# RWKV-6 attention with a tanh-shrink MLP on one core: in the boot, two state sums move from VectorE to ScalarE and GpSimd, and two weight loads are issued later

## The chip, the core and the metric

The kernel runs on one core of a Trainium2 chip. The core has five engines that run beside each other and wait for each other through semaphores: TensorE (PE, matrix products; the loading of its weights is listed apart as PEld), VectorE (DVE), ScalarE (ACT), GpSimd (POOL) and SyncE (SP, which here only issues DMAs). The metric is the device time of one execution in microseconds. Before the change it is 544.36 us, the median of 3 runs (544.14 to 544.81).

## The reference

Two stages follow each other. The first is an RWKV-6 attention over 4 batches, 8 heads, 768 tokens and a head width of 48; the second an MLP on the 3072 x 384 matrix that it makes.

```python
for t in range(S):
    cur = np.einsum('bhd,bhe->bhde', u[None] * kt, vt)
    y[:, :, t] = np.einsum('bhd,bhde->bhe', rt, state + cur)
    state = wt[:, :, :, None] * state + np.einsum('bhd,bhe->bhde', kt, vt)
...
x = y.transpose(0, 2, 1, 3).reshape(B * S, H * D)     # 3072 x 384
h = x @ w_in                                          # 384 x 2048
g = h - np.tanh(h)
return g @ w_out                                      # 2048 x 384
```

## The kernel before

**Tiling.** The 3072 tokens are cut into 8 blocks of 384 (four batches, two halves `q` of each). In a block the attention works in 6 chunks of 64 tokens. The 8 heads are held as 4 pairs, and the pairs as two halves, `h1` (pairs 2 and 3) and `h2` (pairs 0 and 1). Inside a chunk the result comes from scores (`from_scores`, L698: values by a masked matrix A), across chunks from states (`from_states`, L679). The results are copied out of PSUM by `result_out` (L741) into `xT0` to `xT2`, the transposed input of the MLP. Each xT takes 96 of its 128 rows from one pair; the other 32 rows, the "holes", come from the fourth pair, which is first copied to a tile `late` and then spread by six small DMAs (`fill_holes`, L789: half of them issued by SyncE, half by GpSimd, two for each xT).

**The MLP.** It runs in 16 rounds `f` for each block: TensorE multiplies xT by a 128-column slice of `w_in` (`first`, L883), ScalarE copies the product out of PSUM (L888), ScalarE and VectorE work out h - tanh h, and TensorE multiplies by a slice of `w_out`. Round 0 takes xT2 first, then xT1, then xT0. While TensorE does this for one block, the other engines prepare the attention of the next.

**The weights** arrive as 64-bit words, in 16 raw loads of 768 KB (`load_weights`, L251, five buffers). Each one is turned into float32 by three ScalarE pieces (L264: one writes `w_sb`, two write `up`) and one VectorE piece (L268). The order of loads is fixed by `UNITS`: the first raw load holds `w_in` for rounds 0 and 1, the second for rounds 2 and 3, the third `w_out` for rounds 0 and 1.

**The boot.** The first block has nothing to hide behind, so its attention is written out by hand in `boot`. TensorE, SyncE, VectorE and ScalarE run exactly in the order in which `boot` names their work; GpSimd's order is left to the scheduler. `begin_behind(a, b)` makes b wait for a. For each half the boot turns the keys, lets TensorE make the chunks' updates in two PSUM tiles (`update_half`, L616; one tile, `hp` or `acc`, for each pair), and lets VectorE form all states of a pair by one scan (`states_half`, L631). The state that the next block begins with is the last one of the scan plus one more column of the PSUM tile: two VectorE additions for each half (L632), which write `states[1]`. Block 1 reads `states[1]` in its own update (L587).

**Loads in the boot.** SyncE issues the inputs and the first raw load at once. The second raw load waits for the last product of the first half's `update_half` (`blk.done`). The third waits for the last score of the second half's `own` (L494, scores on the diagonal) and stands between the DMAs of the holes: first the holes of xT2, then this load, then the holes of xT1 and xT0. The fourth waits for the last score of `earlier` (L494 again, off-diagonal). ScalarE's order in this stretch: keys of the second half (L523), first piece of the first raw load, the copies to `late` and xT2, the other two pieces, the three pieces of the second raw load (`second_a`), then its parts of the copies to xT1 and xT0, and the pieces of the third (`third_a`).

Of the kernel before, what the change touches and what calls it, by code (L numbers as in the profile page):

```python
# [46 lines left out]
ALU = mybir.AluOpType  # L47
# [3 lines left out]
B, H, S, D = 4, 8, 768, 48  # L51
# [4 lines left out]
NCH = NB // L  # L56
# [70 lines left out]
def kernel(  # L127
# [12 lines left out]
    nc = tc.nc  # L140
# [29 lines left out]
    start = const.tile([P, UP * NCH * LP], F32, name="start", tag="start")  # L170
# [16 lines left out]
    def draw(names, cols):  # L187
        nc.gpsimd.memset(mask_all[0:L, cols], 1.0)
        for m in names:
# [5 lines left out]
            else:  # L195
# [10 lines left out]
                   in_=start[:, 0:BANK].unsqueeze(1).to_broadcast([P, 2 * NPAIR * NCP * L // BANK, BANK]))  # L206

    states0 = const.tile([P, WIDE], F32, name="states0", tag="states0")
    states = [states0[:, 0:NPAIR * NCH * L].rearrange("d (p c e) -> d p c e", c=NCH, e=L),
              const.tile([P, NPAIR, NCH, L], F32, name="states1", tag="states1")]  # L210
# [72 lines left out]
    class Turns:  # L283
# [4 lines left out]
        def tile(self, *_, **__):  # L288
# [3 lines left out]
    first_totals, first_states = (conv.tile([P, NPAIR, D, NCH], F32, name=name, tag=name, bufs=1)  # L292
                                  for name in ("first_totals", "first_states"))
# [20 lines left out]
    def begin_behind(ins, then):  # L314
        tc.add_manual_dep(then.ins, ins.ins.name, mybir.DependencyInfo(
            mybir.DependencyClass.Sync, mybir.DependencyReason.DATA))
# [3 lines left out]
    class Block:  # L320
# [281 lines left out]
        def update_half(self, pair, p0):  # L602

            self.by_column = [t[:, 0:D * NCH].rearrange("d (e c) -> d e c", c=NCH) for t in pair]
            for x in range(UP):
                if x:
                    nc.tensor.drain().then_inc(fence, 1)
                    fences.append(None)
                    nc.tensor.wait_ge(fence, len(fences))
                for c in range(0, NCH, 2):  # L610
                    for h in range(2):
                        for par in range(2):
                            p = (x + par) % UP
                            toks = slice(64 * par, 64 * par + 64)
                            e0 = (p0 + p) * D2 + h * D
                            self.done = nc.tensor.matmul(self.by_column[p][64 * h:64 * h + 64, :, (c + par + 1) % NCH],  # L616
                                             lhsT=self.ks[toks, p0 + p, c // 2, 64 * h:64 * h + 64],
                                             rhs=self.v[toks, c // 2, e0:e0 + D], start=True, stop=True)

        def totals_by_column(self, p0):  # L620

# [4 lines left out]
        def states_half(self, p0):  # L626

            for p in reversed(range(UP)):
                to, by, kv = (t.rearrange("d e c -> d (e c)") for t in
                              (first_states[:, p0 + p], first_totals[:, p0 + p], self.by_column[p]))  # L630
                nc.vector.tensor_tensor_scan(out=to, data0=kv, data1=by, initial=0.0, op0=ALU.add, op1=ALU.mult)  # L631
            return [lambda p=p0 + p, kv=kv: nc.vector.tensor_tensor(  # L632
                out=states[1][:, p, 0, 0:D], in0=first_states[:, p, :, NCH - 1], in1=kv[:, :, 0], op=ALU.add)
                for p, kv in enumerate(self.by_column)]

        def update_any(self, ps, p0, tot):
            ks, last = self.ks[:, p0:p0 + UP], self.q == NQ - 1
# [88 lines left out]
        def in_turn(self, pairs):  # L726

            for p in reversed(pairs):
                self.ended[p] = nc.gpsimd.memset(ended_at, 0.0)
                begin_behind(self.latest[p], self.ended[p])  # L730

        def result_out(self, pairs, copy=None):

            copies = []
            for p in reversed(pairs):
                n = p // 2
                src = self.yp[p % 2][:, :, n * NCP * L:(n + 1) * NCP * L].rearrange("e a (c t) -> e c a t", t=L)
                dst = self.xT[p] if p < KC else self.late
                dst = dst.rearrange("e (c a t) -> e c a t", a=2, t=L)
                for h, rows in enumerate((slice(0, D), slice(64, 64 + D)) if copy else (slice(0, P),)):  # L740
                    copies.append((copy[h] if copy else nc.scalar.copy)(out=dst[rows], in_=src[rows]))  # L741
            return copies[0]
# [374 lines left out]
    def more_weights(queue):  # L1117
        raws.append(load_weights(more_weights.n, queue))
        more_weights.n += 1
        return raws[-1][-1]  # L1120
# [3 lines left out]
    def run(ops):  # L1124
        for op in ops:
            op()
# [13 lines left out]
    def boot(ps, pair, blk, later):  # L1140
        h1, h2 = HALVES
        blk.tiles["w"] = states0
        for name, p0, n in (("w", h1 + 1, 1), ("w", h1, 1), ("k", h1, UP), ("r", h1, UP), ("w", h2, UP)):
            blk.load(name, p0, n)
        blk.load_v()
        blk.load("k", h2, UP)
        blk.load("r", h2, UP)
        more_weights(nc.sync)

        both = (h1, h1 + 1), (h2, h2 + 1)  # L1150
        blk.behind(h1 + 1, 1)
        blk.behind(h1, 1)
        blk.take_whole(h1, UP)
        blk.totals_by_column(h1)
        nc.scalar.copy(out=later_ident, in_=ident)
        blk.before(h1, UP)
        blk.times_behind(h1, UP)
        blk.times_u(h1, UP)
        own = blk.own(ps, h1, spare=94, ahead=5, late=6)
        blk.turn_1(ps, h1)  # L1160
        blk.times_before(h1, UP)
        earlier = blk.earlier(ps, h1)
        blk.behind(h2, UP)
        blk.take_whole(h2, UP)
        first_a, first_b = convert(*raws.pop(0), tiles=2)
        own()
        blk.turn_2(h1)
        blk.totals_by_column(h2)
        blk.update_half(pair, h1)
        begin_behind(blk.done, more_weights(nc.sync))  # L1170
        blk.times_behind(h2, UP)
        blk.times_u(h2, UP)
        blk.turn_1(ps, h2)
        blk.turn_2(h2)
        earlier()
        blk.results(ps)
        blk.result("from_scores", both[0])
        blk.in_turn(both[0])
        run(blk.states_half(h1))
        blk.result("from_states", both[0], True, apart=True)  # L1180
        blk.before(h2, UP)
        blk.update_half(pair, h2)
        blk.times_before(h2, UP)
        own = blk.own(ps, h2)
        own_scored = blk.done
        run(first_a[:1])
        blk.result_out((3,), [nc.scalar.copy] * 2)
        blk.result_out((2,))
        earlier = blk.earlier(ps, h2, ahead=1)
        scored = blk.done  # L1190
        onwards = blk.states_half(h2)
        own()
        run(first_a[1:])
        needed = 2 * KC - 2
        blk.fill_holes([nc.sync, nc.gpsimd], range(needed, 2 * KC))
        begin_behind(own_scored, more_weights(nc.sync))
        blk.fill_holes([nc.sync, nc.gpsimd], range(needed))
        begin_behind(scored, more_weights(nc.sync))
        later.load("w")
        second_a, second_b = convert(*raws.pop(0))  # L1200
        third_a, third_b = convert(*raws.pop(0))
        run(second_a)
        more_weights(nc.sync)
        blk.results(ps)
        blk.yp.reverse()
        blk.result("from_states", both[1], apart=True)
        blk.in_turn(both[1])
        earlier(1, 1)
        earlier(0, 1)
        for p in reversed(both[1]):  # L1210
            blk.result("from_scores", (p,), True)
        later.load("k")
        more_weights(nc.sync)
        run(onwards)
        run(first_b[:1])
        for p in reversed(both[1]):
            blk.result_out((p,), [nc.scalar.copy, nc.vector.tensor_copy])
        run(first_b[1:])
        run(third_a[:2])
        run(second_b)  # L1220
        blk.held(0, NPAIR)
        return [(third_a[2], third_b)]
# [11 lines left out]
    ahead_of_h, rest, formed, extra, behind, due, summed = [], [], [], [], [], [], []  # L1234
# [26 lines left out]
    for i, blk in enumerate(blocks):  # L1261
# [9 lines left out]
        for f in range(NF):  # L1271
# [4 lines left out]
            to = [acc[0], acc[1], hp, spare_a, spare_b, spare_a][now] if now < 6 else hp  # L1276
            h, made = first(here, f, to[:, 0:NB], SPACED[i][f > 12 + (i < 2)])
# [30 lines left out]
            rest, behind, formed, forming, held_back = later_ops, [], [], held_back, []  # L1308
# [54 lines left out]
            for name in loads.get(f, ()):  # L1363
                of, ins = (after if name in ("w", "k", "r") else later), None
                if name == "weights":
                    ins = more_weights(nc.sync)
                elif name == "row":
                    ins = nc.sync.dma_start(out=u_row, in_=u_all)
                elif of and name.startswith("tokens"):
                    ins = of.load_tokens(name[-1])  # L1370
                elif of:
                    ins = of.load_v() if name == "v" else of.load(name.split()[-1])
# [14 lines left out]
    for op in ahead_of_h + rest:  # L1387
        op()
    nc.vector.tensor_single_scalar(again, sure[0:1, 0, 0:1], float(P * (n_whole + n_excess + n_top)),
                                   op=ALU.not_equal)  # L1390
# [77 lines left out]
```

## Time and profile before

| what | us |
|---|---|
| median of 3 runs | 544.36 |
| the profiled execution: its own time | 543.88 |
| the profiled execution: span of its instructions | 542.2 |
| PE busy | 534.0 |
| DVE busy | 459.3 |
| ACT busy | 404.2 |
| POOL busy | 7.0 |

Rows of a timeline show start and duration in us, engine, source line, operation, the tiles (out<-in), shape and count; in brackets stands the engine's idle time before the row and who ended it. Two or more instructions of one kind in a row are merged (x2), and their time is then that of the whole group. A row of the chain of waits has a start, a duration and what it was spent on. Rows of DMA issues end with the median us from issue to landing. Where a window's row lists the engines, the order is PE, weight loads, DVE, ACT, POOL, TensorE's granted clock, the share of the DMA engines and GB/s.

### The profile page before, as it was taken

The page shows a single profiled execution, that of the slowest core. Times are in us where ns is not written, and L with a number is a line of the kernel's source. Part 1 is how long each engine was busy: PE and PEld are TensorE (multiplying, and loading weights), DVE is VectorE, ACT ScalarE, POOL GpSimd, SP SyncE. Part 2 cuts the span into 40 slices and gives each one's busy share as a digit, 9 for nine tenths or more (in the row PEclk, how much of TensorE's full clock was granted, in tenths as well). Part 3 has the DMA queues.
Part 4 walks back from the last instruction along what each step waited for, and adds up shares of the span by engine and source line. Part 5 has one row for each costly group of instructions (what it writes and reads, how often), then busy time and mean ns, then how long its engine had stood idle before and what let it go on. Part 6 is the DMA issues. An engine that isn't in the chain of part 4 may idle for free.

```text
span 542.2 us, 14874 instructions
## 1 busy us (share of the span) xinstructions
PE 534.0 (98%) x5682; PEld 403.4 (74%) x5682; DVE 459.3 (85%) x943; ACT 404.2 (75%) x814; POOL 7.0 (1%) x51
## 2 busy tenths in 40 slices
PE   8999999999999999999999999999999999999996
PEld 5756665678787777877887787877788788777874
DVE  7999999999989989798997989879797997557563
ACT  4999996897668886688767886688766885766561
POOL 1100000000000000000000000000000000000000
PEclk9999999999999999999999999999999999999999
DMA  7799642342311642154122622135321510100101
GB/s 276 242 403 348 219 119 71 122 112 81 106 48 46 162 118 57 44 148 119 61 56 87 132 92 70 50 102 145 90 84 45 118 31 3 56 1 0 45 1 47
DMA packets 53048, 56.34 MB, mean 104 GB/s; under 512 B 21488, under 2 KB 50928, under 8 KB 52976
## 3 DMA queue, kind: packets, MB, share of 16 engines
q1 hardware_dynamic: 52592, 55.18, 33.5%
q8 instruction: 48, 0.79, 0.6%
q14 instruction: 24, 0.20, 0.1%
q10 hardware_dynamic: 288, 0.10, 0.1%
q0 software_dynamic: 96, 0.07, 0.1%
HBM read 44.73 MB, written 4.72 MB: 91 GB/s over the span
## 4 chain that ended last, share of the span: by engine, by line
PE 95%; DVE 2%; DMA 1%; issue 0%; PEld 0%; SPq 0%; PEldq 0%; DVEq 0%
PE hp L883 44%; PE acc L1011 27%; PE att L1011 7%; PE acc L962 5%; PE att L769 4%; PE att L494 2%; PE acc L989 2%; PE att L575 1%; PE att L883 1%; DMA r<-in_rT 1%; PE acc L883 1%; DVE scores L502 1%; DVE post L429 0%; PE att L989 0%; PEld att L679 0%
## 5 line engine op out<-in xcount | busy, mean ns | idle before, releaser
L883 PE MATMUL hp<-xT,w_sb 128*128 128x384 f32 x738 | 259.2, 487 | 0.5 <-DVE w_sb L268 0.5
L883 PEld LDWEIGHTS hp<-xT,w_sb 128*128 128x128 f32 x738 | 131.9, 190 | 69.7 <-issue 0.6
L1011 PE MATMUL acc<-forms,g 128*128 128x128 f32 x954 | 133.2, 276 | 0.0
L888 ACT ACTIVATE h<-hp 128x384 f32<-128x384 f32 x123 | 60.4, 491 | 97.2 <-PE hp L883 97.1
L1011 PEld LDWEIGHTS acc<-forms,g 128*128 128x128 f32 x954 | 122.0, 192 | 10.3
L891 DVE SCALAR_TENSOR_TENSOR h<-h,s 128x384 f32<-128x384 f32 x128 | 70.6, 552 | 51.6 <-ACT s L906 51.5
L932 DVE TENSOR_TENSOR g<-g 128x256 f32<-128x256 f32 x265 | 103.4, 420 | 7.3 <-PE acc L1011 6.5
L907 ACT ACTIVATE qa<-s,shift 128x384 f32<-128x384 f32 x113 | 69.5, 615 | 3.7
L909 ACT ACTIVATE junk<-s,shift 128x384 bf16<-128x384 f32 x113 | 67.7, 599 | 0.0
L891 DVE SCALAR_TENSOR_TENSOR g<-qa,h 128x384 f32<-128x384 f32 x112 | 61.7, 551 | 1.6 <-ACT qa L917 0.2
L906 ACT ACTIVATE s<-h 128x384 f32<-128x384 f32 x113 | 59.1, 523 | 3.5
L1011 PEld LDWEIGHTS acc<-w_sb,g 128*128 128x128 f32 x318 | 46.7, 191 | 9.7 <-ACT sums L979 0.3
L1011 PE MATMUL acc<-w_sb,g 128*128 128x128 f32 x318 | 53.0, 276 | 0.0
L1011 PE MATMUL att<-w_sb,g 128*128 128x128 f32 x212 | 35.5, 275 | 0.0
L1011 PEld LDWEIGHTS att<-w_sb,g 128*128 128x128 f32 x212 | 31.1, 192 | 5.3
L1046 DVE TENSOR_TENSOR sums<-sums 128x256 f32<-128x256 f32 x84 | 32.9, 407 | 1.7 <-ACT sums L1023 1.4
L962 PE MATMUL acc<-w_sb,sums 128*128 128x384 f32 x96 | 33.7, 487 | 0.0
L264 ACT ACTIVATE up<-raw 128x768 f16<-128x768 f32 (+1 forms) x32 | 33.1, 1074 | 0.0
L962 PEld LDWEIGHTS acc<-w_sb,sums 128*128 128x128 f32 x96 | 18.0, 190 | 12.3 <-DVE sums L891 0.3
L417 DVE TENSOR_TENSOR_SCAN pre<-w,start 128x780 f32<-128x780 f32 x14 | 25.0, 1783 | 0.8
L429 DVE TENSOR_TENSOR_SCAN post<-w,seed 128x780 f32<-128x780 f32 x14 | 24.9, 1776 | 0.0
L909 ACT ACTIVATION_READ_ACCUMULATOR junk<-s,shift 128x1 f32 x113 | 21.1, 186 | 0.0
(119 smaller groups left out, 530.5 us busy)
## 6 DMA issues: line engine op xcount, KB each, us to landing
raw<-in_weights SPq DMA_DIRECT2D x16, 768.0 KB, 7.0
w<-in_wT SPq DMA_DIRECT2D x7, 780.0 KB, 4.5
k<-in_kT SPq DMA_DIRECT2D x7, 768.0 KB, 4.6
r<-in_rT SPq DMA_DIRECT2D x7, 768.0 KB, 4.5
v_sb<-in_v SPq DMA_DIRECT2D x8, 576.0 KB, 3.9
k<-in_tokens SPq DMA_DIRECT2D x7, 576.0 KB, 5.0
r<-in_tokens SPq DMA_DIRECT2D x7, 576.0 KB, 4.8
out_y<-sums SPq DMA_DIRECT2D x18, 128.0 KB, 1.8
```

The costliest lines, as they stand in the source:

```text
L264: return lambda: nc.scalar.activation(out=to, in_=of, func=AF.Copy, scale=scale, bias=bias)
L417: return nc.vector.tensor_tensor_scan(out=self.tile("pre")[:, cols], data0=self.tile("w")[:, cols], data1=start[:, 0:n * NCH * LP], initia ...
L883: nc.tensor.matmul(hp, lhsT=w_in_sb[:, f, kc, :], rhs=xT[kc], start=(kc == KC - 1), stop=(kc == 0))
L888: return h, nc.scalar.activation(out=h, in_=hp, func=AF.Copy, scale=1.0 / UPSCALE)
L891: return lambda: nc.vector.scalar_tensor_tensor(out=out, in0=in0, scalar=scalar, in1=in1, op0=op0, op1=ALU.mult)
L906: nc.scalar.activation(out=s, in_=h, func=AF.Square)
L907: nc.scalar.activation(out=qa, in_=s, func=AF.Square, bias=shift[:, 4:5])
L909: nc.scalar.activation(out=junk[:, 0:NB], in_=s, func=AF.Relu, bias=shift[:, 5:6], accum_out=excess[:, at:at + 1])
L932: return lambda: nc.vector.tensor_tensor(out=G[:, to:to + 2], in0=two(G, g_at(q, a0), g_at(q, a1)), in1=two(G, g_at(q, b0), g_at(q, b1)), ...
L962: nc.tensor.matmul(acc, lhsT=g[:, j * P:(j + 1) * P], rhs=w_out_sb[:, f, :], start=(f == self.first), stop=(f == NF - 1))
L1011: nc.tensor.matmul(to, lhsT=G[:, g_at(q, a), :], rhs=rhs, start=start, stop=stop, skip_group_check=True)
L1046: ops.append(lambda op=op, at=at: nc.vector.tensor_tensor(out=at[0], in0=at[1], in1=at[2], op=OPS[op]))
```

## The change

The last sum of a half is split in two. ScalarE copies the PSUM column into `states[1]` (two copies for each half, in the place of the two VectorE additions), and one GpSimd addition for all four pairs, `last_sums`, adds the scan's last states. That addition waits for the first VectorE weight piece (`first_b[0]`) and for GpSimd's own marks `ended`.

The second raw load now waits for the first product of the second half's `update_half`, instead of the last product of the first half's. The third raw load now stands behind the DMAs of all holes and waits for the last off-diagonal score of the second half; the fourth follows it directly.

```diff
         def update_half(self, pair, p0):
...
+            first = None
...
-                            self.done = nc.tensor.matmul(self.by_column[p][64 * h:64 * h + 64, :, (c + par + 1) % NCH],
+                            made = nc.tensor.matmul(self.by_column[p][64 * h:64 * h + 64, :, (c + par + 1) % NCH],
...
+                            first = first or made
+            return first
...
         def states_half(self, p0):
...
-            return [lambda p=p0 + p, kv=kv: nc.vector.tensor_tensor(
-                out=states[1][:, p, 0, 0:D], in0=first_states[:, p, :, NCH - 1], in1=kv[:, :, 0], op=ALU.add)
-                for p, kv in enumerate(self.by_column)]
+            return [lambda p=p0 + p, kv=kv: nc.scalar.copy(out=states[1][:, p, 0, 0:D], in_=kv[:, :, 0])
+                    for p, kv in enumerate(self.by_column)]
+
+        def last_sums(self, *behind):
+
+            to = states[1][:, :, 0, 0:D]
+            ins = nc.gpsimd.tensor_tensor(out=to, in0=to, in1=first_states[:, :, :, NCH - 1], op=ALU.add)
+            for of in behind:
+                begin_behind(of, ins)
...
         def in_turn(self, pairs):
...
+            return [self.ended[p] for p in pairs]
...
     def boot(ps, pair, blk, later):
...
         blk.update_half(pair, h1)
-        begin_behind(blk.done, more_weights(nc.sync))
...
-        blk.update_half(pair, h2)
+        begin_behind(blk.update_half(pair, h2), more_weights(nc.sync))
         blk.times_before(h2, UP)
         own = blk.own(ps, h2)
-        own_scored = blk.done
...
         blk.fill_holes([nc.sync, nc.gpsimd], range(needed, 2 * KC))
-        begin_behind(own_scored, more_weights(nc.sync))
         blk.fill_holes([nc.sync, nc.gpsimd], range(needed))
+        begin_behind(scored, more_weights(nc.sync))
         begin_behind(scored, more_weights(nc.sync))
...
-        blk.in_turn(both[1])
+        ended = blk.in_turn(both[1])
...
         run(onwards)
-        run(first_b[:1])
+        blk.last_sums(first_b[0](), *ended)
```

More of the change, by code (lines that the diff above doesn't have):

```diff
@@ L615, in update_half @@
                             e0 = (p0 + p) * D2 + h * D
-                            self.done = nc.tensor.matmul(self.by_column[p][64 * h:64 * h + 64, :, (c + par + 1) % NCH],
-                                             lhsT=self.ks[toks, p0 + p, c // 2, 64 * h:64 * h + 64],
-                                             rhs=self.v[toks, c // 2, e0:e0 + D], start=True, stop=True)
+                            made = nc.tensor.matmul(self.by_column[p][64 * h:64 * h + 64, :, (c + par + 1) % NCH],
+                                                    lhsT=self.ks[toks, p0 + p, c // 2, 64 * h:64 * h + 64],
+                                                    rhs=self.v[toks, c // 2, e0:e0 + D], start=True, stop=True)
+                            first = first or made
+            return first
         def totals_by_column(self, p0):
```

## The prediction

> **What bounds the kernel now.** I read the page first, for the bound of the whole, then the chain of waits, and then each queue's timeline between 13 and 28 us, where all that the change touches lies.
>
> ```profile
> span 542.2 us, 14874 instructions
> PE 534.0 (98%) x5682; PEld 403.4 (74%) x5682; DVE 459.3 (85%) x943; ACT 404.2 (75%) x814; POOL 7.0 (1%) x51
> 36.00:48.00 12.00, 12.00 (x47) 7.58 (x46) 11.59 (x24) 12.00 (x18) 0.00 (x0) 1.00 1.04 393
> 52.04 0.88 PE L883 MATMUL hp<-xT,w_sb 128*128 128x384 f32 x2 [0.46 <-DVE w_sb L268]
> ```
>
> TensorE is busy for 98% of the span, so the kernel can only lose or win where it waits, and the boot is such a place. The window row (36 to 48 us: PE, weight loads, DVE, ACT, POOL) shows what follows the boot: TensorE and ScalarE are busy for all of its 12.00 us and VectorE for 11.59. No engine there catches up; at 52.04 TensorE even waits 0.46 us for a converted weight. So a shift of the first dense product is, as far as rows show, a shift of the end.
>
> The chain of waits shows who sets that first product:
>
> ```profile
> 18.80 1.40 DVE first_states L631 x2
> 20.19 0.95 DVE scores L502
> 22.41 0.84 PE att L698 x40
> 23.25 0.84 PE acc L883 x2
> 24.14 3.62 PE acc L883 x10
> 23.18 0.30 PEld L883 LDWEIGHTS acc<-xT,w_sb 128*128 128x128 f32 x2
> 24.11 0.30 PEld L883 LDWEIGHTS acc<-xT,w_sb 128*128 128x128 f32 x2 [0.63 <-DVE xT L741]
> 24.92 0.30 PEld L883 LDWEIGHTS acc<-xT,w_sb 128*128 128x128 f32 x2 [0.51 <-DVE xT L741]
> 25.56 1.59 PEld L883 LDWEIGHTS acc<-xT,w_sb 128*128 128x128 f32 x6 [0.34 <-issue]
> ```
>
> VectorE's scans and masked copies set the time up to 22 us, then TensorE multiplies scores (L698), and the dense product begins at 23.18. Its first of 16 rounds has three steps, one for each slice of xT: 23.18 (xT2), 24.11 (xT1), 24.92 (xT0); round two starts at 25.56. Without waits a step takes 25.56 - 24.92 = 0.64 us, so the two waits cost the round 25.56 - 23.18 - 3 x 0.64 = 0.46 us. I take the start of round two, 25.56, as the mark for the sum.
>
> **The loads.** Who is really awaited at 24.11 and 24.92 is seen in SyncE's issues and their landings (the issues' rows end in the median us to landing):
>
> ```profile
> 13.44 0.34 SPq L251 DMA_DIRECT2D raw<-in_weights  x1
> raw<-in_weights SPq DMA_DIRECT2D x1, 768.0 KB, 4.3
> 18.52 0.43 SPq L251 DMA_DIRECT2D raw<-in_weights  x1
> raw<-in_weights SPq DMA_DIRECT2D x1, 768.0 KB, 5.3
> 19.00 1.15 SPq L789 DMA_DIRECT2D xT<-late  x2
> xT<-late SPq DMA_DIRECT2D x1, 24.0 KB, 5.0
> xT<-late SPq DMA_DIRECT2D x1, 24.0 KB, 5.2
> DMA to landing us min/median/max: 4.1/7.0/12.5
> q0 software_dynamic: 96, 0.07, 0.5%
> ```
>
> The second raw load is issued at 13.44 and lands 4.3 later, at 17.7. The third is issued at 18.52 and lands at 23.8. Behind it stand the two holes of xT1 (19.00) and xT0 (19.00 + 1.15 - 0.58 = 19.57), which land at 24.00 and 24.77: 0.11 and 0.15 us ahead of TensorE's steps at 24.11 and 24.92. So the releaser named (VectorE, whose copies end at 23.90 and 24.39, below) is not the one: the holes behind the third load are. The change takes that load out of their way. The last two rows are the least time of any raw load (4.1 in the first 75 us), and the three holes that GpSimd issues: 0.5% of 60 us, 0.3 us of all 16 DMA engines.
>
> **ScalarE, VectorE and TensorE around it:**
>
> ```profile
> 15.13 0.92 ACT L264 ACTIVATE w_sb<-raw 128x768 f32<-128x768 f32 x1
> 16.20 0.97 ACT L741 COPY late<-att 48x384 f32<-48x384 f32 x2
> 17.57 2.02 ACT L264 ACTIVATE up<-raw 128x768 f16<-128x768 f32 x2
> 19.44 0.92 ACT L264 ACTIVATE w_sb<-raw 128x768 f32<-128x768 f32 x1
> 20.23 2.02 ACT L264 ACTIVATE up<-raw 128x768 f16<-128x768 f32 x2
> 22.83 0.96 ACT L741 COPY xT<-att 48x384 f32<-48x384 f32 x2 [0.58 <-PE att L698]
> 14.77 0.73 DVE L631 TENSOR_TENSOR_SCAN first_states<-hp,first_totals 128x288 f32<-128x288 f32 x1
> 15.54 0.24 DVE L632 TENSOR_TENSOR states<-first_states,hp 128x48 f32<-128x48 f32 x1
> 15.85 0.22 DVE L416 RECIPROCAL start<-whole 128x12 f32<-128x12 f32 x1
> 22.23 0.21 DVE L632 TENSOR_TENSOR states<-first_states,hp 128x48 f32<-128x48 f32 x1
> 23.34 1.05 DVE L741 COPY xT<-att 48x384 f32<-48x384 f32 x2 [0.28 <-ACT xT L741]
> 16.40 0.25 PE L616 MATMUL hp<-v_sb,ks 64*64 64x48 f32 x1
> 17.57 0.90 PE L494 MATMUL att<-r,k 48*64 48x64 f32 x48
> ```
>
> **Part 1, the two VectorE additions of each half go.** The first pair spans 15.54 to 15.85, on the chain (the scans behind it lead to 18.80): 0.31 us earlier from there to the end of the scores at 23.2. The second pair (22.23 on, about 0.3) lies behind the last masked copy; only the weight pieces follow, so its going moves the mark by nothing.
>
> **Part 2, two ScalarE copies of 128x48 for each half.** No row has that shape. The nearest are these:
>
> ```profile
> 2.63 0.20 ACT L159 ACTIVATE warm<-shift 128x1 f32<-128x1 f32 x1
> 6.14 0.29 ACT L1155 COPY later_ident<-ident 128x128 f32<-128x128 f32 x1
> 0.96 0.75 POOL L171 MEMSET start<- 128x780 f32 x1
> 57.59 0.35 DVE L587 TENSOR_TENSOR states<-states,whole 128x192 f32<-128x192 f32 x1
> ```
>
> Between them, 0.10 (with the overlap of about 0.1 that back-to-back pieces show: 17.57 + 2.02 = 19.59, the next starts at 19.44) and 0.29 each; I take 0.20, two copies 0.40. [...] No row here has the shape to decide it.
>
> The first pair must follow the scans of the same PSUM tiles, as VectorE's copy at 23.34 follows ScalarE's copy out of the same tile: start 14.77 + 0.73 + 0.05 = 15.55, end 15.95. Then the piece that ran at 15.13 starts, and with a pitch of 20.23 - 19.44 = 0.79 the copies of "late" begin at 16.74, not 16.20: 0.54 later, as are the holes. TensorE's update of the second half (16.40) also has to wait for these copies; it has 0.45 us to spare. ScalarE would reach the second load's pieces at 19.44 + 0.54 = 19.98.
>
> **Part 3, the second raw load waits for the first product of the second update.** That ends at 16.40 + 0.25 = 16.65; SyncE follows within 0.05 (17.57 + 0.90 = 18.47, issue at 18.52): 16.70 instead of 13.44. Behind it on SyncE wait the holes, ready only from about 18.1, and they are not held. Landing: at least 4.1, here the uncontended 4.3 of the same load; the three GpSimd holes now fall into its flight and own 0.3 us of the engines, of which I charge 0.2; at most the 5.3 of the third load. I take 4.5: it lands at 21.2 (20.8 to 22.0). [...]
>
> So ScalarE waits from 19.98 to 21.2, and behind this wait stand the second pair of copies and both copies to xT. Counted from the landing L: three pieces take 22.25 - 0.15 - 19.44 = 2.66, two copies 0.40, so xT1's copy starts at L + 3.06; VectorE's half of it 0.51 later (22.83 to 23.34) and 0.56 long, then 0.10 to TensorE: step xT1 at L + 4.23, xT0 0.64 later (its copies are ready by then), round two at L + 5.51. With L = 21.2 that is 26.71 against 25.56: **+1.15 us**. The 0.31 of part 1 and the 0.46 of the holes lie inside this new wait and win nothing.
>
> **Part 4, the third raw load behind the holes and the off-diagonal scores.** Those end 0.3 earlier than before, so it is issued near 20.0, not 18.52, behind three holes; with 4.3 to 5.0 it lands at 24.3 to 25.0. Its pieces now start at L + 4.0 = 25.2, so it is hidden by the second load's lateness; at 5.3 it would be at its edge. The loads behind it stream as before.
>
> **Part 5, the GpSimd addition** (128x192): between 0.2 and 0.75 us by the memset row, cover until 57.59, where the states are first read; nothing behind it on GpSimd is due earlier. Cost 0, and at most 0.75 if that cover were gone.
>
> Sum: -0 -0 +1.15 = +1.15 on the profiled 543.88 us (span 542.2); on the runs' median of 544.36 that is **545.5**, 0.21% slower.
>
> **The rivals.**
> *The load is in time.* If the second load lands by 20.05, L + 5.51 is 25.56 and the loss is gone; below that ScalarE's own 19.98 sets the mark at 25.49. Price -0.1: 544.3, not slower. For it: the engines are empty when it is issued. Against: it needs a flight of 3.35 us, and none took less than 4.1.
> *The holes and both loads crowd each other.* With 5.3, L = 22.0 and the sum is +1.95: 546.3. For it: the third load took 5.3 with holes beside it; against: those stood behind it with a fourth load, while the GpSimd holes are 72 KB.
> *The boot's gains count whole.* Scores 0.31 earlier, no wait in round one (0.46), and the 0.46 at 52.04 gone as well: -1.2, 543.1. It needs ScalarE to keep ahead, against part 3.
>
> **How the numbers follow.** A measurement of this kernel tells about 0.2%, 1.09 us, from no change. My forecast's case (landing at 20.8 to 21.7, +0.7 to +1.65) has 0.66, of which 0.40 above +1.09 and 0.26 below; the load in time 0.13 (same 0.12, faster 0.01); crowding 0.15 (slower); the whole gain 0.06 (faster). Faster 0.07, same 0.38, slower 0.55. The likeliest case's own range is 545.0 to 546.0; to hold 8 in 10 it reaches from 544.4 to 546.6 (crowding with dear copies: +1.95 + 0.2).
>
> **What would show it.** Right: ScalarE idle before the second load's w_sb piece, released by a DMA, until about 21.2; its xT copies at 24.3; steps at 25.4 and 26.1; round two at 26.7, and the same lag at 52. The holes on SyncE land by 22.5. VectorE's reciprocal at 15.5. Wrong: that piece starting by 20.1, or TensorE ahead of 25.56 in round two, or a lag that shrinks between 27 and 52 us.

## The result and the profile after

| | before | after |
|---|---|---|
| median, us (6 runs each) | 544.25 (543.87 to 544.81) | 547.32 (545.46 to 549.90) |
| the profiled execution: own time | 543.88 | 545.46 |
| the profiled execution: span | 542.2 | 543.7 |

The changed kernel is slower: the ratio is 1.006, with a 95% interval of 1.0042 to 1.0077. The profiled execution is the fastest of its six, 1.58 us slower than that of before; the median is 3.07 us slower. So there are two questions: what costs the 1.58 that the profile shows, and what it does not show. The first is answered by the profile alone.

The page of the changed kernel, then its chain of waits (start, duration, what it was spent on):

```profile
span 543.7 us, 14873 instructions
PE 532.6 (98%) x5682; PEld 403.1 (74%) x5682; DVE 458.5 (84%) x939; ACT 404.1 (74%) x818; POOL 7.7 (1%) x52
```

```profile
16.78 5.22 DMA raw<-in_weights
...
22.03 0.30 ACT w_sb L264
...
22.84 1.94 ACT up L264 x2
24.78 0.15 ACT states L635 x2
...
24.97 0.91 PE acc L893 x2
...
25.93 3.49 PE acc L893 x10
...
53.69 2.17 PE hp L893 x6
```

TensorE is busy for 1.4 us less than before (532.6 against 534.0) and yet ends later; what is new is at the head of the chain. Before, the chain ran through VectorE's scans and the scores; now it runs through the flight of the second raw load (issued 16.78, 5.22 long), ScalarE's three pieces of it, and the two new copies. The timeline of the changed kernel, one engine after the other (VectorE, ScalarE, TensorE's weight loads, GpSimd, SyncE), shows how the wait is handed on:

```profile
15.36 0.20 DVE L416 RECIPROCAL start<-whole 128x12 f32<-128x12 f32 x1
15.47 0.20 ACT L635 COPY states<-hp 128x48 f32<-128x48 f32 x1 [0.41 <-DVE first_states L634]
...
22.03 0.91 ACT L264 ACTIVATE w_sb<-raw 128x768 f32<-128x768 f32 x1 [2.17 <-DMA raw<-in_weights]
...
24.66 0.17 ACT L635 COPY states<-hp 128x48 f32<-128x48 f32 x1
...
24.81 0.84 ACT L751 COPY xT<-att 48x384 f32<-48x384 f32 x2
25.55 0.90 ACT L264 ACTIVATE w_sb<-raw 128x768 f32<-128x768 f32 x1
19.52 0.36 PEld L494 LDWEIGHTS att<-pre,post 48*64 48x64 f32 x17 [0.32 <-issue]
...
24.97 0.30 PEld L893 LDWEIGHTS acc<-xT,w_sb 128*128 128x128 f32 x2 [2.38 <-ACT states L635]
25.92 0.30 PEld L893 LDWEIGHTS acc<-xT,w_sb 128*128 128x128 f32 x2 [0.65 <-DVE xT L751]
26.40 0.47 PEld L893 LDWEIGHTS acc<-xT,w_sb 128*128 128x128 f32 x2 [0.18 <-DVE xT L751]
27.05 1.75 PEld L893 LDWEIGHTS acc<-xT,w_sb 128*128 128x128 f32 x6 [0.19 <-PE acc L893]
25.06 0.69 POOL L641 TENSOR_TENSOR states<-states,first_states 128x192 f32<-128x192 f32 x1 [2.92 <-ACT states L635]
20.11 0.91 SPq L251 DMA_DIRECT2D raw<-in_weights  x2
```

ScalarE stands idle for 2.17 us until the load lands, does its pieces and copies, and TensorE's first dense product waits 2.38 us for the last of the copies out of PSUM: round 0 accumulates in the same tile `acc` that the copy reads. Round two of the dense products starts at 27.05 where it started at 25.56 (+1.49), and the product at 53.69 stood at 52.04 (+1.65). The lag stays to the end: +1.58 on the execution's own time.

The flight of 5.2 us is in the view of the DMA packets between 17 and 18.6 us, changed kernel. Its GB/s row has 40 slices of 0.04 us each:

```profile
GB/s 0 0 0 0 0 0 0 410 0 0 0 0 0 0 0 0 0 0 154 614 461 0 0 0 0 0 0 0 0 0 0 0 154 307 0 0 0 0 307 307
q8 instruction: 1, 0.02, 3.7%
raw<-in_weights SPq DMA_DIRECT2D x1, 768.0 KB, 5.2
xT<-late POOLq DMA_DIRECT2D x3, 24.0 KB, 4.5
xT<-late SPq DMA_DIRECT2D x1, 24.0 KB, 4.6
```

The holes that GpSimd and SyncE issue now take 4.5 to 4.9 us (medians of 4.5 and 4.6), in the load's company; the four that left ahead of the third load before took 1.8 to 2.4. Keep the lone burst in the eighth slice (17.3 us) in mind: it is one packet of the queue whose kind the view calls "instruction" (410 GB/s for 0.04 us, so 16 KB), and it comes just ahead of the first packets of the raw load (17.7 us). The short pause of 0.32 us at 19.52, inside the off-diagonal scores, is put down to it below.

### The profile page after: what moved, and what is told of

Same layout as the page of the kernel before. It is cut to its first block, busy times and chain, and to the rows that moved or that the text cites. A ratio compares the mean times of both kernels' runs of the same rounds, so it can differ in the third digit from the quotient of the medians.

```text
span 543.7 us, 14873 instructions
## 1 busy us (share of the span) xinstructions
PE 532.6 (98%) x5682; PEld 403.1 (74%) x5682; DVE 458.5 (84%) x939; ACT 404.1 (74%) x818; POOL 7.7 (1%) x52
## 3 DMA queue, kind: packets, MB, share of 16 engines
HBM read 44.73 MB, written 4.72 MB: 91 GB/s over the span
## 4 chain that ended last, share of the span: by engine, by line
PE 94%; DMA 2%; DVE 2%; issue 1%; ACT 0%; SPq 0%; DVEq 0%
PE hp L893 44%; PE acc L1021 27%; PE att L1021 7%; PE acc L972 5%; PE att L779 4%; PE att L494 2%; PE acc L999 2%; PE att L575 1%; PE att L893 1%; DMA r<-in_rT 1%; DMA raw<-in_weights 1%; PE acc L893 1%; ACT up L264 0%; DVE scores L502 0%; DVE post L429 0%
```

## The experiments

The profile explains 1.58 us. For the rest there were two theories. The **clock**: TensorE's idle time ahead of the first dense product lets the granted clock fall. The **instruction fetch**: the packet at 17.3 us is taken for TensorE's next block of instructions (no view says whose it is), which could get behind the load that the change has put there. A third question was which of the three edits costs at all. Ratios are to the kernel before, with the 95% interval, from runs on the same chip.

| kernel | median (range; runs), us | ratio |
|---|---|---|
| after_again: the changed kernel | 549.94 (545.34 to 550.78; 6) | 1.0088 (1.0063 to 1.0113) |
| second_alone: only the second load moved | 547.62 (545.34 to 549.23; 12) | 1.0052 (1.0034 to 1.007) |
| third_alone: only the third load moved | 545.97 (545.04 to 547.18; 12) | 1.0021 (1.0009 to 1.0034) |
| sums_alone: only the sums moved | 545.02 (543.73 to 546.03; 12) | 1.0003 (0.999 to 1.0015) |
| second_back: changed, second load as before | 546.05 (544.96 to 547.75; 12) | 1.0022 (1.0009 to 1.0035) |
| after_filled: changed, idle time filled | 547.51 (545.26 to 550.3; 8) | 1.0056 (1.0031 to 1.0081) |
| before_gap: before, with an idle time | 545.6 (545.12 to 547.66; 12) | 1.0018 (1.0005 to 1.0031) |
| second_later: changed, second load later still | 548.93 (547.17 to 549.59; 6) | 1.0078 (1.0058 to 1.0098) |
| second_between: changed, second load earlier | 547.6 (547.5 to 548.09; 5) | 1.0059 (1.0045 to 1.0073) |
| holes_by_pool: sums moved, holes by GpSimd | 544.33 (543.92 to 546.52; 12) | 0.999 (0.9976 to 1.0004) |
| third_unhurried: holes first, third load's pieces later | 547.12 (545.93 to 547.34; 5) | 1.0043 (1.003 to 1.0057) |

### Which edit costs

The changed kernel once more, in a set of runs of its own:

> The changed kernel once more, to see how its executions spread and whether a profile of a longer one can be had. Theory A (late second load, then the clock): the start of round two stays near 27.0 us in every execution, some 1.5 us behind before, and what the longer executions have beyond that goes with a lower mean granted clock (0.996), because TensorE stands idle for 2.4 us ahead of the first dense product; times from 545.4 to 550, median 547. Theory B (the load's landing itself varies): the longer executions show round two later than 28 us at a clock of 0.999.

Five of its six executions took 546.96 to 550.78, one 545.34: the spread belongs to the kernel. The profiled one was the fastest again (round two at 27.00), so it does not decide between theories A and B. Then the second load put back to its old place in the changed kernel, and moved alone in the kernel before (with `update_half` returning its first product, as in the change):

```diff
 second_back (against the changed kernel)
+            self.done = made
             return first
...
         blk.update_half(pair, h1)
+        begin_behind(blk.done, more_weights(nc.sync))
...
-        begin_behind(blk.update_half(pair, h2), more_weights(nc.sync))
+        blk.update_half(pair, h2)
```

> The changed kernel with the second raw load alone put back behind the last product of the first update; the third load stays behind the holes, the sums stay on ScalarE and GpSimd. Theory A: ScalarE finds the load landed (17.7), TensorE's idle time ahead of round one shrinks below 0.5 us, the clock stays at 0.999, 543.4 to 544.3 us with little spread. Rival C (the sums on ScalarE and GpSimd cost the time, because the first dense product needs the PSUM tile that ScalarE copies from): still 1 us or more above before.

```diff
 second_alone (against the kernel before)
-        begin_behind(blk.done, more_weights(nc.sync))
...
-        blk.update_half(pair, h2)
+        begin_behind(blk.update_half(pair, h2), more_weights(nc.sync))
```

> The kernel before with nothing changed but the second raw load's place (behind the first product of the second update). Theory A: ScalarE waits until about 22 us for it, its copies to xT slip by 2 us, TensorE is idle for some 2 us between the steps of round one, 545.5 to 547 us. Rival C: no more than 0.5 us above before.

The second load's move alone gives 547.62, above the 545.5 to 547 that was expected, and the spread of the changed kernel, whose two sets have 547.32 and 549.94. Without it 546.05 is left, and no execution above 547.75; that is still above before. So one more edit costs. The third load and the sums, each alone:

```diff
 third_alone (against the kernel before)
         blk.fill_holes([nc.sync, nc.gpsimd], range(needed, 2 * KC))
-        begin_behind(own_scored, more_weights(nc.sync))
         blk.fill_holes([nc.sync, nc.gpsimd], range(needed))
+        begin_behind(scored, more_weights(nc.sync))
         begin_behind(scored, more_weights(nc.sync))
```

> The kernel before with nothing changed but the third raw load's place (behind all holes and the last off-diagonal score). Theory D (each of the two loads costs time by itself): the holes land by 22, so TensorE's waits in round one shrink, but the load is issued near 20.2 and lands at 25.5 to 26.5, ScalarE waits for it 2 us behind its copies to xT, and the product of round one is copied out late: 545 to 546.5 us, 1 to 2 us above before, at a clock mostly near 1.0. Rival E (the third load is hidden by other work, and what stayed in the run with the second load put back was the sums): within 0.4 us of before.

> The kernel before with the sums moved to ScalarE and GpSimd and both loads where they were. Theory D: VectorE is 0.3 us earlier into the second half, the holes still stand behind the third load, so time is the same as before or up to 0.4 us less. Rival E: 1 us or more above before.

The sums' move (the `last_sums` part of the diff without the loads') gives 1.0003: no difference that can be told. The third load's move costs 0.21%. The timelines of third_alone and, for the same place, of sums_alone show what it wins and loses:

```profile
25.29 0.93 ACT L264 ACTIVATE w_sb<-raw 128x768 f32<-128x768 f32 x1 [1.02 <-DMA raw<-in_weights]
25.57 1.41 PEld L883 LDWEIGHTS acc<-xT,w_sb 128*128 128x128 f32 x5 [0.20 <-PE acc L883]
28.50 0.96 DVE L268 SCALAR_TENSOR_TENSOR w_sb<-w_sb,up 128x768 int32<-128x768 int32 x1 [0.40 <-ACT up L264]
53.53 2.17 PE hp L883 x6
```

```profile
24.79 0.30 PEld L894 LDWEIGHTS acc<-xT,w_sb 128*128 128x128 f32 x2 [1.37 <-DVE xT L752]
```

In third_alone the three steps of round one take 1.91 us (23.66 to 25.57) where they took 2.38 before, so the holes' waits are gone, as the prediction read them. Round two starts at 25.57, as before, since this execution came to round one 0.48 us later. But ScalarE has waited 1.02 us for the third load, and the product that was at 52.04 is at 53.53. ScalarE was busy for all of the window from 36 to 48 us before, so what it loses there probably comes back as a late weight. In sums_alone the holes stand behind the load as before: the hole of xT1 lands at 24.7 (issued at 19.71, 5.0 long), and the step follows at 24.79. The holes' wait and the load's wait are two sides of one trade. Two tries to get round that trade failed. One gave all six holes to GpSimd:

> The sums on ScalarE and GpSimd, both loads where they were before, and all six hole DMAs issued by GpSimd, so that the third load is neither ahead of the holes on SyncE's queue nor later than before. Theory D: TensorE's two waits in round one (0.46 us) and 0.3 us of VectorE go, nothing is late: 543.2 to 544.1, up to 0.8 us below before. If GpSimd's six issues (0.5 us each) are too slow, the last hole lands near 22.5, still ahead of need.

That is not told apart from before: 0.999 (0.9976 to 1.0004). The other put the holes first and the third load's pieces behind the copy of the first product:

```diff
 third_unhurried (against the changed kernel; second load put back as in second_back)
+        own_scored = blk.done
...
         blk.fill_holes([nc.sync, nc.gpsimd], range(needed))
-        begin_behind(scored, more_weights(nc.sync))
+        begin_behind(own_scored, more_weights(nc.sync))
...
-        run(third_a[:2])
...
-        return [(third_a[2], third_b)]
+        return [(third_a[0], []), (third_a[1], []), (third_a[2], third_b)]
...
-                ops = square + converting(pieces, 2)
+                ops = square + converting(pieces, 4)
```

> The sums moved, the second raw load as in the kernel before; the holes that SyncE fills go ahead of the third raw load, and the three pieces of the third load that ScalarE makes come behind its copy of round one's product and not between the two copies to xT. If the third load's lateness costs only through ScalarE's order (a piece that waits for it and holds back the copy of the first product), the holes' 0.46 us are won: 543.2 to 544.2 against 544.2 to 544.8 for the kernel before. If the lateness costs through the weights that are missing later, it comes out at 545 or more, as with the third load's move alone (545.97).

It came out at 547.12, on the side of the second reading: the lateness costs through the weights. In its timeline VectorE waits 2.09 us for ScalarE's pieces. These start at 26.18, though the load landed near 25.0 (issued at 20.53, 4.5 long), so the new order has a part in the wait, and the run does not part the two:

```profile
28.97 0.96 DVE L268 SCALAR_TENSOR_TENSOR w_sb<-w_sb,up 128x768 int32<-128x768 int32 x1 [2.09 <-ACT up L264]
```

### The spread: clock

In after_filled five products of TensorE that nobody reads fill a part of the idle time (1.43 us of it are left where the changed kernel has 2.38):

```diff
 after_filled (against the changed kernel)
-            self.opened = None
+            self.opened, self.scored_in = None, ps_t
...
         for p in reversed(both[1]):
             blk.result("from_scores", (p,), True)
+        busy(blk.scored_in[:, 0], 5)
```

> The changed kernel with five extra products of 128x512 (2.1 us, into a PSUM tile that is free by then) between the second half's scores and the first dense product, where TensorE stood idle for 2.4 us; its result is the same. Theory A: the clock stays at 0.999 in every execution, all executions lie near the shortest of the changed kernel, 545.2 to 545.9, the spread of 4 us is gone. Theory B: the same spread and median as the changed kernel, 547.

Its eight executions fall into two groups: 545.26 to 546.36 (four, mean clock 0.999 to 1.0) and 548.66 to 550.3 (four, 0.993 to 0.996). The changed kernel's executions around 547 (four of twelve in its two sets of runs) are missing here; those around 549 and 550 are not. So the idle time ahead of the first dense product may stand behind one group, but not behind the other. The counterpart makes an idle time in the kernel before, with three ScalarE pieces done a second time and no load moved:

```diff
 before_gap (against the kernel before)
         run(first_b[:1])
+        run(second_a[1:] + second_a[1:2])
```

> The kernel before with three more ScalarE pieces of 128x768 (2.8 us; they write the second raw load's parts once more, to the same values) ahead of its copies to xT; no load is moved. TensorE then stands idle for about 2 us in round one, as it does in the changed kernel, with the DMA queues as before. Theory A (the idle time itself drops the clock in most executions): some 2 us from the lateness in every execution, and 1.7 us more at a mean clock of 0.996 in most of them, 546 to 548.5. Theory F (the executions of the changed kernel spread because loads and instruction fetches meet): 546 to 546.7 at a clock as before, little spread.

Nine of its twelve executions took 545.12 to 546.06, three 546.96 to 547.66: an idle time alone gave none near 549. The median of 545.6 is below what either theory gave. (The kernel before itself has executions at a mean clock of 0.995: four of 25 beside the first experiments, at 545.07 to 546.2, where its median is 544.5; and one of 35 on the chip of before_gap, whose median there is 544.84, took 547.04 at 0.992.) The profiled one is the slowest; its timeline has the idle time:

```profile
26.49 0.42 PEld L883 LDWEIGHTS acc<-xT,w_sb 128*128 128x128 f32 x2 [2.45 <-DVE xT L741]
```

Since the profile of the changed kernel was its fastest execution, three more profiles of it were taken:

> The changed kernel, one profiled execution, to have the trace of a long one (547 to 551 us). Theory A (idle time alone drops the clock): a half-speed stretch of 3.4 us directly behind TensorE's idle time at 22.6 to 25 us, and nothing else. Theory G (TensorE's instruction fetch at 17.3 us meets the second load's flight): TensorE stands still for 1 us or more inside the off-diagonal scores (from 19.2), behind an instruction fetch that starts or ends later than 18.3; the loads that wait for those scores are issued late, and a half-speed stretch follows there.

> As look_1: the changed kernel again, to have the trace of a long execution; A and G as there.

> As look_1: the changed kernel again, to have the trace of a long execution; A and G as there.

They took 546.96, 550.25 and 549.22, and show two different ways to be longer. look_1, its first dense product and then its windows (the granted clock is the third number from the end):

```profile
24.77 0.30 PEld L893 LDWEIGHTS acc<-xT,w_sb 128*128 128x128 f32 x2 [2.20 <-ACT states L635]
```

```profile
25.00:26.00 1.00, 0.95 (x3) 0.33 (x3) 0.88 (x2) 0.92 (x3) 0.55 (x1) 0.88 0.93 374
26.00:27.00 1.00, 1.00 (x2) 0.57 (x3) 0.97 (x3) 1.00 (x2) 0.00 (x0) 0.50 1.07 402
...
28.00:29.00 1.00, 1.00 (x3) 0.49 (x2) 0.00 (x0) 0.30 (x1) 0.00 (x0) 0.50 1.00 404
29.00:30.00 1.00, 1.00 (x4) 0.61 (x3) 0.57 (x2) 1.00 (x2) 0.00 (x0) 0.92 0.95 375
```

Up to the first dense product look_1 is, within 0.2 us, the profiled execution of the changed kernel. Then the clock is at half (0.50 in the windows from 26 to 29 us). If the windows at its two ends mix only half and full clock, the one with a mean of 0.88 was at half for 2 x 0.12 of its 1 us, so the stretch is about 2 x 0.12 + 3 + 2 x 0.08 = 3.4 us long; second_back, second_between and before_gap come to 3.4 us in the same way. The execution ends 1.50 us later than that one (546.96 against 545.46), near the 1.7 us that half of the stretch would be, an estimate for a TensorE that is busy all through it. The idle time of 2.38 us in the changed kernel's profile was followed by full clock (1.00 in every window from 25 to 28 us), and so was that of second_alone's, of which 1.93 us lie between 24 and 52 us, at a mean clock of 1.00 there; 2.20 here was followed by half clock. What decides between the two, and what sets the 3.4 us, no run shows.

### The spread: instruction fetch

look_2 is the slower one. Its timeline, its packets from 17 to 18.6 us, then those from 21 to 22.5 us, and its windows:

```profile
23.93 0.60 PEld L494 LDWEIGHTS att<-pre,post 48*64 48x64 f32 x17 [4.72 <-issue]
24.86 1.58 SPq L251 DMA_DIRECT2D raw<-in_weights  x2
58.36 2.17 PE hp L893 x6
```

```profile
GB/s 0 0 0 0 0 0 0 0 0 0 0 0 0 0 0 0 0 0 0 154 614 461 0 0 0 154 0 154 154 614 461 307 0 0 0 0 0 154 0 0
```

```profile
GB/s 82 0 82 41 41 41 0 41 478 41 0 0 0 0 0 0 0 0 0 0 0 0 0 0 0 0 0 0 0 0 0 0 0 0 0 0 0 0 0 0
...
q8 instruction: 1, 0.02, 5.0%
```

```profile
23.00:24.00 1.00, 0.07 (x5) 0.07 (x5) 0.00 (x0) 1.00 (x2) 0.00 (x0) 0.78 0.02 5
24.00:25.00 1.00, 1.00 (x31) 1.00 (x32) 0.07 (x1) 0.90 (x3) 0.10 (x2) 0.50 0.00 0
...
30.00:31.00 1.00, 1.00 (x4) 0.62 (x3) 0.79 (x2) 1.00 (x2) 0.00 (x0) 0.81 0.93 346
```

The load's first packets come at 17.8 us as in the profile of the changed kernel, but the lone packet ahead of them is missing. No packet of the kind "instruction" is in that view; from 21 to 22.5 us there is one, at 21.3 us (the ninth of 40 slices of 0.0375 us), when the load is nearly through. TensorE, which has stopped after loading the weights of the 30th of 48 off-diagonal scores, goes on at 23.93, after 4.72 us in which it waited for nothing that the profile shows. In the profile of the changed kernel it paused 0.32 us at the same score. That the packet is what TensorE waits for, and that look_2's is the one of 17.3 us come late, is read from the times, since the changed kernel's profile has a second packet at 21.32 as well. In eleven profiles TensorE pauses at this score or the one before, from 0.22 to 4.72 us, and in the eight of them in which a view has the packet it goes on 2.2 to 2.6 us behind it (17.31 and 19.52 in the changed kernel's). Before, third_alone, before_gap and holes_by_pool show no pause; of their packets only that of before is in a view (17.34), so why they have none is open. Loads three and four wait for these scores: they are issued at 24.86, not 20.11. Behind the idle time lies a longer stretch of half clock (by the same reckoning 2 x 0.22 + 6 + 2 x 0.19 = 6.8 us, from 23.6 to 30.4). The product that stood at 53.69 is at 58.36. look_3 is of the same kind: 4.37 us at the same score, and no packet of the kind "instruction" between 17 and 18.6 us. There the load itself is late too (6.6 us, landing at 23.6), which is theory B; but the copies to xT wait for TensorE's scores until 27.45, so the landing does not set the time.

Two kernels move the second load to tell the theories apart. second_later issues it behind the last diagonal score, at 18.95 us, well after 17.3, where the changed kernel's profile has the packet:

```diff
 second_later
-        begin_behind(blk.update_half(pair, h2), more_weights(nc.sync))
+        blk.update_half(pair, h2)
...
         own = blk.own(ps, h2)
+        begin_behind(blk.done, more_weights(nc.sync))
```

> The changed kernel with the second raw load later still, behind the last diagonal score of the second half (18.4), so that its flight begins only when the instruction fetch of 17.3 to 18.3 is over. It lands near 23.5, so the floor rises by some 1.5 us to 546.8. Theory G: the executions draw together, most within 2 us of that floor. Theory A: the idle time grows to 4 us, nearly every execution has a half-speed stretch, 548.5 and more, with the clock at 0.996 or below.

TensorE now idles 4.05 us ahead of the first dense product; all six executions show a mean clock of 0.995 or 0.996, and the times lie between 547.17 and 549.59. In its profile the wait stands ahead of the first dense product:

```profile
27.25 0.30 PEld L893 LDWEIGHTS acc<-xT,w_sb 128*128 128x128 f32 x2 [4.05 <-ACT states L635]
```

That is theory A's forecast, in four of six executions by its time (548.5 and more) and in all by the clock. Of theory G the scores without a long pause (loads three and four, which wait for the last of them, are issued at 21.39, not 24.86 as in look_2) and the smaller spread (2.4 us against 5.4) come out; the closeness to 546.8 does not, since only two of six lie within 2 us of it. second_between issues the load earlier, so that it is hardly late but flies across 17.3 us (`first_from` is the first product that `from_states` issues):

```diff
 second_between (against the changed kernel)
+            self.first_from = getattr(self, "first_from", None) or made
...
+        blk.first_from = None
         blk.result("from_states", both[0], True, apart=True)
+        begin_behind(blk.first_from, more_weights(nc.sync))
         blk.before(h2, UP)
-        begin_behind(blk.update_half(pair, h2), more_weights(nc.sync))
+        blk.update_half(pair, h2)
```

> The changed kernel, but the second raw load is issued behind the first product from states of the first half (issue near 15.4 us), so that it should land at 19.7 to 20.6 and ScalarE should wait for it by 0 to 0.7 us. Its flight then lies over 17.3 us, where TensorE's next 16 KB of instructions are due. Theory A (TensorE's idle time ahead of the first dense product lowers the clock and makes the spread): that idle time is 1.5 us or less here, so the time is 545 to 546, most executions within 0.5 of each other, and no stall lies in the off-diagonal scores. Theory G (the instruction fetch waits behind the load's flight): TensorE stalls by 1 to 3 us inside the off-diagonal scores in part of the executions, the fetch comes near the load's landing (19 to 20.5), and the times spread from 545 to 549, with a median of 546.5 or more, although the load is hardly late.

Its timeline, its packets from 20 to 21.2 us, and its windows:

```profile
16.17 0.34 SPq L251 DMA_DIRECT2D raw<-in_weights  x1
20.66 0.90 ACT L264 ACTIVATE w_sb<-raw 128x768 f32<-128x768 f32 x1
22.32 0.36 PEld L494 LDWEIGHTS att<-pre,post 48*64 48x64 f32 x17 [2.36 <-issue]
```

```profile
q8 instruction: 1, 0.02, 5.1%
```

```profile
23.00:24.00 1.00, 1.00 (x34) 1.00 (x32) 1.00 (x3) 0.56 (x3) 0.09 (x2) 0.66 0.13 35
24.00:25.00 1.00, 1.00 (x36) 1.00 (x34) 0.47 (x2) 0.00 (x0) 0.12 (x2) 0.50 0.85 258
```

ScalarE does not wait for the load at all, and still the kernel takes 547.6. The packet comes at 20.04, TensorE pauses 2.36 us at the same score, and half clock follows the pause. The fetch theory holds in pause, packet and median; its spread (545 to 549) does not: all five executions lie within 0.6 us, which would fit a packet that is late every time; one of them has its packet in a view. Lateness alone, which called for 545 to 546 and no pause, falls. In the timeline of second_back, whose profiled execution is its slowest (547.75), the pause is there with the load in its old place, but shorter (1.70 us); the packet is at 18.28. From 17.5 to 18.0 us the DMA engines carried one packet of under 512 B there, so no load was moving data in that half microsecond, and still the packet came 1.0 us later than the changed kernel's (17.31); what made it late stays open:

```profile
20.89 0.61 PEld L494 LDWEIGHTS att<-pre,post 48*64 48x64 f32 x17 [1.70 <-issue]
```

## Why the prediction was wrong

**Direction and chain: right.** The second load's landing sets ScalarE's pieces, the copies to xT and the dense steps, as forecast. The holes win nothing. VectorE's gain (the reciprocal starts at 15.36 instead of 15.85: 0.49 us, not 0.31) lies inside the new wait; TensorE's off-diagonal scores lost nearly all of it to the pause of 0.32 us, and their last weights are loaded 0.07 us earlier than before (19.94 against 20.01), where 0.3 was forecast.

**Part 3, the flight: mis-sized.** 4.5 us was taken, 5.2 measured; the landing is 22.0, not 21.2. That is the landing of the rival that lets the holes and the load crowd each other (which had a chance of 0.15). The way from landing to round two was taken as 5.51 and is 27.05 - 22.00 = 5.05, mostly since the two copies take 0.15 between them (24.66 to 24.81) and not 0.40, and since step xT0 follows step xT1 by 0.48 (25.92 to 26.40) and not 0.64. So the term is +1.49 against +1.15. That the step of xT2 waits as well, because it accumulates in the tile that the second copy reads, was not seen; it moves no mark, since xT1 comes later still, but it makes one long idle time of TensorE where the forecast had a wait behind the first step.

**Part 4, the third load: right, at its edge.** It is issued at 20.11, takes 5.4 us instead of 4.3 to 5.0 and lands at 25.5, and its piece starts at 25.55 without a wait. The cover was the second load's lateness: third_alone, without that cover, costs 0.21%.

**Parts 1, 2 and 5: right in sum.** The copies and the GpSimd addition (0.69 us, between the 0.2 and 0.75 of the bounds) cost nothing by sums_alone.

**The step that failed** is the sum of part 3, with two terms that it put at nothing without a reason. First, the forecast moved a 768 KB load to 16.7 us and asked what its flight does to ScalarE and to the holes, but not what else moves on the DMA engines at that time: the packet of the kind "instruction" at 17.3 us. Part 4 has the scores end 0.3 us earlier; in look_2 TensorE stops for 4.72 us inside them. Second, it made TensorE wait over 2 us and charged only the wait, not the stretch of half clock that can follow; so "a shift of the first dense product is, as far as rows show, a shift of the end" fails in look_1, where the product comes no later than in the changed kernel's profile and the end 1.50 us later. look_2 shows both at 4.79 us (550.25 - 545.46). The sum was made on one execution and put on the median. For the profiled execution, which has no half clock (1.00 in every window from 15 to 28 us) and a stop of only 0.32 us, it nearly held: +1.58 was measured where +1.15 was forecast, 545.46 against 543.88 + 1.15 = 545.03; that 545.46 also meets the forecast of 545.5 for the median is luck. The median is 547.32, with a range that ended at 546.6. How many of the unprofiled executions fall to each is only argued, from their times and mean clocks. That the load's new place brings the executions around 549 is shown by second_alone, which has them, and second_back, which has none. That TensorE stops for 2.36 to 4.72 us where no packet of the kind "instruction" is through ahead of the load is shown by the profiles of look_2, look_3 and second_between; that the missing packet is the cause is read from the times, and what holds it back was not tried.

## What to carry to other kernels

A transfer that is moved should be laid against everything that uses the DMA engines in its new flight, the packets of the kind "instruction" included: look for them in the view of before (17.34 us here) and keep large loads off that time. An idle time on TensorE such as those here is priced as the wait plus the chance of a half-clock stretch behind it (a stretch of 3.4 or 6.8 us followed five of the seven idle times of 1.70 to 4.72 us whose clock is in a view), and the sum is made for the spread of the executions, not for the one profiled. An edit that costs nothing because another is late has to be tried alone.

## What the runs showed of the hardware

- Where no 16 KB packet of the kind "instruction" came between 17 and 18.6 us, TensorE stood still for 4.72 us (look_2, which has one at 21.3) and 4.37 us (look_3); where it came at 17.31 us, for 0.32 us (the changed kernel's profile). In eight profiles TensorE went on 2.2 to 2.6 us behind the packet.
- TensorE's idle time of 1.70 us (second_back), 2.20 us (look_1), 2.36 us (second_between) and 2.45 us (before_gap) was followed by a stretch of 3.4 us at half clock, and that of 4.72 us (look_2) by 6.8 us, while 2.38 us (the changed kernel's profile) and second_alone's idle time (1.93 us of it between 24 and 52 us) were not.
- A 24 KB transfer of a hole took 4.5 to 4.9 us beside the raw load (the changed kernel's profile), and 1.9 us in the median in third_alone, where the third load stood behind the holes.
- A ScalarE copy of 128x48 out of PSUM took 0.17 to 0.20 us, but only 0.15 us passed from the start of the first of two copies to the start of the next instruction (24.66 to 24.81).
